# A state-space block on one core: two chained running-sum products per tile in place of three, from the second block on

## The chip, the cores and the metric

The kernel runs on 1 core of one Trainium2 chip. The metric is the device time of one launch in microseconds (us), the median of 3 runs: 468.2 us (467.89 to 468.23). The engines are named as the profile names them: PE (TensorE, matrix products; PEld is its weight load), DVE (VectorE), ACT (ScalarE), POOL (GpSimd), SP (SyncE, here only an issuer of DMAs).

## The reference

Input u has 2048 rows (tokens) of 448 channels. The block is adaptive layer norm, a long convolution, and a gated feed-forward:

```python
mod = (_silu(c) @ w_mod).reshape(c.shape[0], 6, 1, -1)     # sa, ca, ga, sb, cb, gb
h = _layernorm(x, axis=-1) * (1 + ca) + sa
x = x + ga * _A_ref(h, ...)     # y[t] = sum over s <= t of K[t-s] h[s], plus h * Dskip
h = _layernorm(x, axis=-1) * (1 + cb) + sb
x = x + gb * _B_ref(h, ...)     # (silu(h @ w_gate) * (h @ w_up)) @ w_down, hidden width 1792
```

K is the convolution kernel of the state-space part. For these inputs the kernel replaces it, after a test on the device, by the first two terms of a series, K[l] = k0 + k1*l for each channel (the path named `small_path`). Then y[t] needs only running sums over the tokens: k0 times the sum of h, and k1 times a sum weighted with the distance. A running sum inside a tile of 128 tokens is one PE product with a triangular matrix of ones, `tri`; what earlier tiles contribute is one row that is carried from tile to tile.

## The kernel before

The tokens are 16 tiles of 128, in 8 blocks of 2 (`TILES`). After a preamble (`PLAN`, lines 43 to 45, which also does the branch of tiles 0 and 1) the function `run_blocks` runs `ffn` on block b while the branch of block b + 1 is done piece by piece beside it.

`ffn` goes through 14 hidden tiles f = 0..13, here called slots. In slot f, `gate_up(f)` issues 22 products on PE (L758), ACT takes the silu of the first bank (L773), DVE multiplies the second bank by it in place (L788, "the multiply" below), ACT casts the product to `phi` (L795), DVE forms the rest `plo` (L796). Then `down(f - 1)` issues six products that read `phi` and `plo` of the slot before (L808). So PE is two products ahead of the other engines, and needs `phi(f)` only after `gate_up(f + 1)`. In block 0 the weights are split too (L122 to L125, L115 to L117).

The branch pieces hang between these in half slots: `TIMES` gives for each of the two tiles of the next block the half slot h of each stage; h // 2 is the slot, and h % 2 says whether the stage is issued before `down(f - 1)` or after it. Every engine has one queue in program order, so a stage that waits holds back the next slot's silu, multiply and cast on its engine.

The stages of `small_path`: s0 makes h (two DVE operations, L200 and L202); s1 multiplies it by the k0 part `gm0` and the k1 part `gm1` (L957); s2 adds the carried rows `run0` and `run1` to row 0 (L962, L963) and splits the k0 part into two halves `vh` and `vl` (L970, L971) for accuracy; s3 multiplies h by the skip weight `gd` (L976); s4 issues the products with `tri` (L982 to L984) and adds the skip part to x; s5 forms the next carried rows (L1003, L1004), sends them by a small DMA from partition 127 to partition 0 (L1005), and adds both sums to x, the second times the token number `tok` (L1007). In block 0 the k0 part is not split but multiplied at full precision (L995), and DVE does s1 and s3; in block 1 DVE does them too, from block 2 on POOL. After the last stage come the second layer norm of the tile (`n2.stat`, its root on POOL, L185 and L186), `make_xn` (L212 on DVE, L215 and L216 on ACT) and `turn`, a transpose on DVE (L236) with DMAs, which has to be ready in slot 13.

`finish` (L827 to L849) does the last two hidden tiles of the last block in an order of its own. The preamble's `left_over` (L428) sums the k1 part of tiles 0 and 1, from which the first carried row is made (L723).

Of the kernel before, what the change touches and what calls it, by code (L numbers as in the profile page):

```python
# [17 lines left out]
NT = L // 128  # L18
# [17 lines left out]
)  # L36

EXTRA = (1,)

# [12 lines left out]
def f32(ap):  # L52
    return ap.bitcast(F32)
# [3 lines left out]
def tile_kernel(ctx, tc, x, a_re, a_im, b_re, b_im, c_re, c_im, log_dt,  # L57
# [229 lines left out]
    with tc.tile_pool(name="pre", bufs=1) as pre:  # L287
# [47 lines left out]
        for z in range(2):  # L335
# [19 lines left out]
        sca = pre.tile([128, N], F32)  # L355
        h01, v0, v1, hd, h2 = ([pre.tile([128, w], t, name=f"{n}_{q}") for q in range(2)] for n, t, w in
                               (("h", F32, D), ("v0", F32, D), ("v1", F32R, D), ("hd", F32, D), ("h2", F32, 512)))
        qt = {n: pre.tile([128, 512], F32, name="qt" + n) for n in "gcs"}
# [113 lines left out]
        def flag_of():  # L472
# [42 lines left out]
            **{f"D{q}": (lambda q: lambda: sc.activation(diag[q], ident, AF.Copy, scale=n2.of[q][1]))(q) for q in range(2)},  # L515
            "fr1": copy(run1[end], CV[end, 0:D]), "fx": copy(xs[0], DN[0][:, 0:D]),
            "tr0": do(to_channels, 0), "tr1": do(to_channels, 1, (0, 1)), "tr1b": do(to_channels, 1, (2, 3)),
# [203 lines left out]
    def first_rows():  # L721

        ve.tensor_tensor(run0[end], run1[end], DN[1][end, 0:D], op=OP.add)  # L723

# [5 lines left out]
    def gate_0():  # L730

        ve.scalar_tensor_tensor(gm0, gm1, ntok, gm0, op0=OP.mult, op1=OP.add)

    def run_blocks(pools, stages, first=None):
        work, hid = pools.work, pools.hid
        def ffn(ts, fresh, last, todo):
# [148 lines left out]
        for b, ts in enumerate(TILES):  # L885
            todo = {}
            if b + 1 < len(TILES):
# [5 lines left out]
                if b:  # L893
                    for i in nx:
                        at(0, 1, load_x, i)
                stat1, root1, times, *late = TIMES[min(b, 2)]
                st = stages(b)
# [6 lines left out]
                if b == 0 and first is None:  # L904
                    go(EXTRA[0], gate_0)
                    todo["mid"] = [(first_rows, ())]
                    at(0, 1, lambda: sy.dma_start(run[0:1], run[127:128]))
                for i, h in zip(nx, stat1):
# [32 lines left out]
    def small_path(pools):  # L941
# [9 lines left out]

        def s1(i, on_v=False):
            h = vs[i]
            v0 = v0_of(i)
            v1 = work.tile([128, D], F32R, name="v1", bufs=2)
            for v, g in ((v0, gm0), (v1, gm1)):
                (ve if on_v else po).tensor_tensor(v, h, g, op=OP.mult)  # L957
            vs[i] = h, v0, v1

        def rows(i):  # L960
            h, v0, v1 = vs[i]
# [3 lines left out]
        def s2(i):
            rows(i)
            h, v0, v1 = vs[i]
            vh = work.tile([128, D], F32R, name="vh")
            vl = work.tile([128, D], F32R, name="vl")
            sc.copy(vh, v0)  # L970
            ve.tensor_tensor(vl, v0, f32(vh), op=OP.subtract)  # L971
            vs[i] = h, vh, vl, v1

        def s3(i, on_v=False):
            h = vs[i][0]
            (ve if on_v else po).tensor_tensor(h, h, gd, op=OP.mult)  # L976

        def s4(i):
            h, vh, vl, v1 = vs[i]
# [5 lines left out]
            ve.tensor_tensor(xs[i], h, xs[i], op=OP.add)
            vs[i] = o, s

        def s4f(i):  # L990
            h, v0, v1 = vs[i]
            o = CV[:, 0:D]
            s = bank()[:, 0:D]
            pe.matmul(s, tri, v1, start=True, stop=True)
            pe.matmul(o, f32(tri), v0, start=True, stop=True)  # L995
            s3(i, True)
            ve.tensor_tensor(xs[i], h, xs[i], op=OP.add)
            vs[i] = o, s

        def s5(i):  # L1000
            o, s = vs.pop(i)
            if i + 1 < NT:
                sc.copy(run1[end], s[end])  # L1003
                ve.scalar_tensor_tensor(run0[end], run1[end], 128.0, o[end], op0=OP.mult, op1=OP.add)  # L1004
                (sy if i in TILES[1] else sc).dma_start(run[0:1], run[127:128])  # L1005
            ve.tensor_tensor(xs[i], xs[i], o, op=OP.add)
            ve.scalar_tensor_tensor(xs[i], s, tok, xs[i], op0=OP.mult, op1=OP.add)  # L1007
# [109 lines left out]
```

## Time and profile before

| | |
|---|---|
| median of 3 runs | 468.2 us (467.89 to 468.23) |
| the profiled execution: its own time | 466.79 us |
| its span, the stretch that the trace covers | 465.0 us |
| PE busy | 455.5 us, 98% |
| DVE, ACT, POOL busy | 293.5, 170.6, 74.4 us |
| granted TensorE clock | 0.998 of full speed |
| chain that ended last | PE 94%, of which L758 60% and L808 28% |

A row of the timeline or of a chain gives the start in us from the span's start, then the duration. The chain is followed back from the last instruction; if it lies on one engine from end to end, time leaves the kernel only by taking work from that engine or by ending its waits. PE's queue reads blocks as: block 0 from 31.6 us, block 1 from 88.4, block 2 from 141.8, block 3 from 195.2, and so on each some 53.3 us, the last ending at 461.

### The profile page before, as it was taken

What the parts mean: (1) busy time and instruction counts of PE and PEld (TensorE: products, weight loads), DVE (VectorE), ACT (ScalarE), POOL (GpSimd) and SP (SyncE); (2) the same over time, 40 slices, a digit from 0 to 9 for tenths busy, and PEclk for the clock granted to TensorE, in tenths of its full rate; (3) what the DMA queues carried; (4) which work ended last, traced back from release to release, by engine and by line L of the source; (5) the groups of instructions that cost most, each with busy time, mean ns of one, the idle gap of its engine ahead of it and who ended that gap; (6) DMA issues with size and microseconds to landing.
All of it is one profiled execution on the core that took longest, in us unless ns stands there. A gap on an engine that the chain in (4) does not pass through costs nothing.

```text
span 465.0 us, 8481 instructions
## 1 busy us (share of the span) xinstructions
PE 455.5 (98%) x3339; PEld 433.7 (93%) x3339; DVE 293.5 (63%) x600; ACT 170.6 (37%) x426; POOL 74.4 (16%) x99
## 2 busy tenths in 40 slices
PE   6899999999999999999999999999999999999996
PEld 4579999999999999999999999999999999999995
DVE  5888999778726676457736766467745775353224
ACT  5889566522333233322323233322323223232121
POOL 1232001001000521023210431014210331000000
PEclk9999999999999999999999999999999999999999
DMA  8965652110112001120112001120012001110001
GB/s 313 406 254 191 211 179 95 45 36 2 47 45 81 1 0 58 36 79 2 43 51 80 1 0 47 47 80 0 26 56 65 27 2 45 47 61 23 1 1 45
DMA packets 20946, 32.92 MB, mean 71 GB/s; under 512 B 2848, under 2 KB 15264, under 8 KB 20896
## 3 DMA queue, kind: packets, MB, share of 16 engines
q1 hardware_dynamic: 20256, 32.10, 19.9%
q8 instruction: 28, 0.46, 0.4%
q10 hardware_dynamic: 640, 0.18, 0.2%
q14 instruction: 22, 0.18, 0.1%
HBM read 25.40 MB, written 6.82 MB: 69 GB/s over the span
## 4 chain that ended last, share of the span: by engine, by line
PE 94%; issue 2%; DVE 1%; DMA 1%; ACT 1%; POOL 0%; DVEq 0%; POOLq 0%; ACTq 0%
PE bank L758 60%; PE dn L808 28%; DMA vec<-in_c_log_dt_dram 1%; PE dn L480 1%; PE cv L982 1%; PE bank L983 1%; PE cv L984 1%; PE bank L266 0%; PE bank L403 0%; PE cv L995 0%; PE bank L437 0%; ACT L339 0%; DVE x L824 0%; PE cv L375 0%; DVE dn L823 0%
## 5 line engine op out<-in xcount | busy, mean ns | idle before, releaser
L758 PE MATMUL bank<-hhi,gu 128*128 128x256 f32 x1568 | 216.7, 278 | 0.1
L758 PEld LDWEIGHTS bank<-hhi,gu 128*128 128x128 f32 x1568 | 204.0, 188 | 3.7 <-issue 0.8
L758 PE MATMUL bank<-hlo,gu 128*128 128x256 f32 x896 | 138.8, 277 | 0.0
L758 PEld LDWEIGHTS bank<-hlo,gu 128*128 128x128 f32 x896 | 118.6, 188 | 0.2
L788 DVE TENSOR_TENSOR bank<-raw,bank 128x256 f32<-128x256 f32 x97 | 41.4, 426 | 98.3 <-PE bank L758 85.5
L795 ACT CAST phi<-bank 128x256 fp32r<-128x256 f32 x111 | 41.4, 373 | 139.8 <-DVE bank L788 139.8
L796 DVE TENSOR_TENSOR plo<-bank,phi 128x256 fp32r<-128x256 f32 x111 | 47.0, 424 | 44.0 <-ACT phi L795 44.0
L773 ACT ACTIVATE raw<-bank 128x256 f32<-128x256 f32 x98 | 37.6, 384 | 93.0 <-PE bank L758 89.2
L808 PE MATMUL dn<-wdh,phi 128*128 128x448 f32 x220 | 62.7, 366 | 0.0
L808 PE MATMUL dn<-wdh,plo 128*128 128x448 f32 x220 | 62.2, 363 | 0.0
L808 PE MATMUL dn<-wdl,phi 128*128 128x448 f32 x220 | 61.7, 362 | 0.0
L808 PEld LDWEIGHTS dn<-wdh,plo 128*128 128x128 f32 x220 | 41.2, 188 | 3.0 <-DVE plo L796 0.3
L808 PEld LDWEIGHTS dn<-wdl,phi 128*128 128x128 f32 x220 | 41.2, 187 | 2.7
L808 PEld LDWEIGHTS dn<-wdh,phi 128*128 128x128 f32 x220 | 34.3, 188 | 1.6 <-ACT phi L795 0.9
L185 POOL TENSOR_SCALAR rsb<-mvb 128x1 f32<-128x1 f32 (+1 forms) x15 | 8.8, 585 | 115.4 <-DVE mvb L157 115.4
L185 POOL TENSOR_SCALAR rsa<-mva 128x2 f32<-128x2 f32 x8 | 2.7, 341 | 134.0 <-DVE mva L157 131.7
L125 DVE TENSOR_TENSOR gu<-raw,gu 128x1024 fp32r<-128x1024 f32 x14 | 17.1, 1220 | 0.9 <-ACT gu L123 0.9
L215 ACT ACTIVATE raw<-raw,rsb 128x64 f32<-128x64 f32 x14 | 4.9, 349 | 34.6 <-POOL rsb L186 33.6
L957 POOL TENSOR_TENSOR m<-m,gm 128x448 f32<-128x448 f32 x10 | 11.6, 1155 | 25.6 <-DVE m L202 25.6
L963 DVE TENSOR_TENSOR v<-v,run 1x448 fp32r<-1x448 f32 x14 | 13.3, 951 | 0.0
L971 DVE TENSOR_TENSOR vl<-m,vh 128x448 fp32r<-128x448 f32 x12 | 7.4, 618 | 8.9 <-ACT vh L970 8.8
L976 POOL TENSOR_TENSOR m<-m,gd 128x448 f32<-128x448 f32 x10 | 12.9, 1294 | 0.4
(237 smaller groups left out, 413.5 us busy)
## 6 DMA issues: line engine op xcount, KB each, us to landing
raw<-in_B_w_gate_up_dram SPq DMA_DIRECT2D x14, 512.0 KB, 3.4
rawd<-in_B_w_down_dram SPq DMA_DIRECT2D x16, 224.0 KB, 3.7
xd<-raw SPq DMA_DIRECT2D x12, 256.0 KB, 2.0
raw<-xd SPq DMA_DIRECT2D x48, 64.0 KB, 2.0
x<-in_A_u_dram SPq DMA_DIRECT2D x12, 224.0 KB, 2.9
out_dram<-x SPq DMA_DIRECT2D x11, 224.0 KB, 2.0
wm<-in_w_mod_groups_dram SPq DMA_DIRECT2D x5, 448.0 KB, 8.2
wm<-in_w_mod_groups_dram SPq DMA_DIRECT2D x5, 336.0 KB, 8.2
```

What stands on the lines that cost most here:

```text
L125: ve.tensor_tensor(wgu[j][:, :, 3:7, :], w[:, :, ::-1, :], f32(wgu[j][:, :, 0:4, :][:, :, ::-1, :]), op=OP.subtract)
L185: po.tensor_scalar(rs[:, 0:n], self.mv[:, 0:n, 1], EPS, None, op0=OP.add)
L758: pe.matmul(ps[s][:, 0:n], w[:, s, a], (hlo if lo else hhi)[:, k, first_col(n):first_col(n) + n], start=first and q == 0, stop=end and q = ...
L773: sc.activation(p[:, 0:n], ps[0][:, 0:n], AF.Silu)
L788: ve.tensor_tensor(ps[1][:, 0:n], p[:, 0:n], ps[1][:, 0:n], op=OP.mult)
L795: sc.copy(hi[:, 0:n], ps[1][:, 0:n])
L796: ve.tensor_tensor(lo[:, 0:n], ps[1][:, 0:n], f32(hi[:, 0:n]), op=OP.subtract)
L808: pe.matmul(dn[q][:, 0:D], u[:, cs], v, start=f == 0 and z == 0, stop=f == (NF - 3 if last else NF - 1) and z == 2)
L957: (ve if on_v else po).tensor_tensor(v, h, g, op=OP.mult)
L963: ve.tensor_tensor(v1[0:1], f32(v1[0:1]), run1[0:1], op=OP.add)
L971: ve.tensor_tensor(vl, v0, f32(vh), op=OP.subtract)
L976: (ve if on_v else po).tensor_tensor(h, h, gd, op=OP.mult)
```

## The change

From block 1 on a tile has eight stages in place of six. s2 adds the carried row of the h sums to h itself, casts it (`hh`) and keeps the small rest in h. s4 issues one product, u = tri x hh, the running sum of h. s5 forms w = k1 * u + k0 * rest (with the second carried row), carries u's last row, and adds gma * u to x, where gma = gm0 - gm1. s6, two slots later, issues the second product v = tri x w, a running sum of the running sum; s7 carries its last row and adds v to x. The skip part and the k0 part of the rest are products and a sum on POOL in s1 and s3; s5 has one more POOL sum. Each carried row has its own ACT copy and its own DMA on ACT's queue.

In block 0 the stages a1 to a4 run both sums on h and apply k1 behind the sum: one DVE product goes from a1, ACT gets a cast there, and a4 gets one DVE product. `rows_0` (POOL in slot 1, DVE and DMA in slot 2) and `rows_1` (slot 1 of block 1) convert the carried rows between the two forms. The preamble gets two ACT casts, `hh0` and `hh1`, and `left_over` sums these. `finish` issues all products of hidden tile 12 first and then all of tile 13.

```diff
-    ((2, 3), 3, ((4, 5, 7, 8, 10, 11, 12), (7, 8, 13, 14, 16, 17, 18))),
-    ((2, 3), 3, ((4, 5, 7, 8, 10, 11, 12), (7, 8, 13, 14, 16, 17, 18))),
+    ((2, 3), 3, ((4, 4, 6, 6, 8, 8, 12, 12, 13), (6, 7, 12, 12, 14, 14, 18, 18, 19))),
...
-EXTRA = (1,)
+EXTRA = (1, 2, 4, 3)
...
-                pe.matmul(CV[:, 0:D], all1, v1[q], start=q == 0, stop=q == 1)
+                pe.matmul(CV[:, 0:D], all1, hh[q], start=q == 0, stop=q == 1)
...
+    def rows_0(part):
+        t = v0_of(2)[end]
+        if part == 0:
+            po.tensor_tensor(t, run1[end], gm1[end], op=OP.mult)
+        else:
+            ve.tensor_tensor(run0[end], run0[end], t, op=OP.add)
+            sy.dma_start(run[0:1], run[127:128])
...
-                sums(NF - 2, range(m))
-                sums(NF - 1, (0,))
-                sums(NF - 2, (m,))
-                sums(NF - 1, range(1, m + 1))
-                sums(NF - 2, (m + 1,))
-                sums(NF - 1, (m + 1,))
+                for f in (NF - 2, NF - 1):
+                    sums(f, range(m + 2))
...
+        def a4(i):
+            o, s, t = vs.pop(i)
+            sc.copy(run1[end], s[end])
+            ve.tensor_tensor(t, s, gm1, op=OP.mult)
+            ve.scalar_tensor_tensor(run0[end], t[end], 128.0, o[end], op0=OP.mult, op1=OP.add)
+            sy.dma_start(run[0:1], run[127:128])
+            ve.tensor_tensor(xs[i], xs[i], o, op=OP.add)
+            ve.scalar_tensor_tensor(xs[i], t, tok, xs[i], op0=OP.mult, op1=OP.add)
...
+        def s2(i):
+            h = vs[i]
+            ve.tensor_tensor(h[0:1], h[0:1], run1[0:1], op=OP.add)
+            hh = work.tile([128, D], F32R, name="hh", bufs=2)
+            sc.copy(hh, h)
+            ve.tensor_tensor(h, h, f32(hh), op=OP.subtract)
...
+        def s3(i):
+            h = vs[i][0]
+            po.tensor_tensor(h, h, gm0, op=OP.mult)
+            po.tensor_tensor(xs[i], xs[i], v0_of(i), op=OP.add)
...
+        def carry(i, k, row):
+            if i + 1 < NT:
+                sc.copy(run[end, k, :], row[end])
+                sc.dma_start(run[0:1, k, :], run[127:128, k, :])
...
+            ve.tensor_tensor(t, u, gm1, op=OP.mult)
+            ve.tensor_tensor(w, t, h, op=OP.add)
+            ve.tensor_tensor(w[0:1], f32(w[0:1]), run0[0:1], op=OP.add)
+            carry(i, 1, u)
+            ve.tensor_tensor(t, u, gma, op=OP.mult)
+            po.tensor_tensor(xs[i], xs[i], t, op=OP.add)
```

PE, block 3, around the first sum of its first prepared tile (tile 8). Before, slot 5, between `gate_up(5)` and `down(4)`:

```order
L758 MATMUL bank<-hhi,gu_509 128x256 x7
L758 MATMUL bank<-hlo,gu_509 128x256 x4
L982 MATMUL cv<-vh,tri 128x448
L983 MATMUL bank<-v_2526,tri 128x448
L984 MATMUL cv<-vl,tri 128x448
L808 MATMUL dn_68<-wdh_558,phi 128x448
```

Now the first sum of tile 8 stands in slot 4 (the sum of `w` follows in the same way in slot 6, as one L1039):

```order
L774 MATMUL bank<-hhi,gu_476 128x256 x7
L774 MATMUL bank<-hlo,gu_476 128x256 x4
L1017 MATMUL cv<-hh,tri 128x448
L824 MATMUL dn_68<-wdh_516,phi 128x448
L824 MATMUL dn_69<-wdh_516,phi 128x448
```

Three products in one place have become one in each of two places; PE has 12 instructions fewer in all (six blocks, two tiles), and no bank of the four that `gate_up` turns through is taken for a sum.

DVE, block 3, from the last stage of tile 8 (x_74) to the multiply of slot 8; m is the buffer of h and of the products, raw the buffer of `make_xn` and also of silu's result. Before:

```order
L212 SCALAR_TENSOR_TENSOR raw<-x_74,mvb,cbw 128x448 [waits DVE_49]
L962 TENSOR_TENSOR m_79<-m_79,run 1x448 [waits DMAHW2_49,Pool_49]
L963 TENSOR_TENSOR v_2604<-v_2604,run 1x448 [waits Pool_49]
L971 TENSOR_TENSOR vl<-m_79,vh 128x448 [waits Activation_49]
L788 TENSOR_TENSOR bank<-raw,bank 128x256 [waits PE_49,Activation_49]
L796 TENSOR_TENSOR plo<-bank,phi 128x256 [waits Activation_49]
L236 STREAM_TRANSPOSE raw<-raw 128x4x4x32
L788 TENSOR_TENSOR bank<-raw,bank 128x256 [waits PE_49,Activation_49]
```

Now:

```order
L1045 TENSOR_TENSOR x_74<-x_74,dn_70 128x448 [waits Activation_49,Pool_49]
L1003 TENSOR_TENSOR m_79<-m_79,run 1x448 [waits DMAHW6_49]
L1006 TENSOR_TENSOR m_79<-m_79,hh 128x448 [waits Activation_49]
L156 BN_STATS stb<-x_74 128x6
L157 BN_AGGR mvb<-stb 128x2 [waits DVE_49]
L804 TENSOR_TENSOR bank<-raw,bank 128x256 [waits PE_49,Activation_49]
L812 TENSOR_TENSOR plo<-bank,phi 128x256 [waits Activation_49]
L212 SCALAR_TENSOR_TENSOR raw<-x_74,mvb,cbw 128x448 [waits DVE_49]
L1029 TENSOR_TENSOR m_79<-cv,g_90 128x448 [waits PE_49,Pool_49]
L1030 TENSOR_TENSOR w<-m_79 128x448 [waits DVE_49]
L1031 TENSOR_TENSOR w<-w,run 1x448 [waits DMAHW7_49,DVE_49]
L1033 TENSOR_TENSOR m_79<-cv,gma 128x448 [waits Activation_49]
```

The transpose L236 and the multiply of slot 8 follow directly. POOL, block 3, from tile 9's h to tile 8's root (L185, L186) and beyond, before:

```order
L957 TENSOR_TENSOR m_79<-m_79,gm_91 128x448 [waits DVE_49,Activation_49]
L957 TENSOR_TENSOR v_2604<-m_79,g_90 128x448 [waits PE_49]
L185 TENSOR_SCALAR rsb<-mvb 128x1 [waits DVE_49]
L186 TENSOR_TENSOR rsb<-rsb,halves 128x1 [waits Pool_49]
L976 TENSOR_TENSOR m_79<-m_79,gd 128x448
```

and now, from tile 9's s1:

```order
L999 TENSOR_TENSOR m_79<-m_79,gd 128x448 [waits DVE_49]
L1034 TENSOR_TENSOR x_74<-x_74,m_79 128x448 [waits DVE_49,Pool_49]
L1011 TENSOR_TENSOR m_79<-m_79,gm_91 128x448 [waits DVE_49]
L1012 TENSOR_TENSOR x_75<-x_75,m_79 128x448 [waits DMAHW5_49,Pool_49]
L185 TENSOR_SCALAR rsb<-mvb 128x1 [waits DVE_49,Activation_49]
L186 TENSOR_TENSOR rsb<-rsb,halves 128x1 [waits Pool_49]
L1034 TENSOR_TENSOR x_75<-x_75,m_79 128x448 [waits DVE_49]
```

The whole second half of the tile's work, four operations of s5, now stands between `make_xn` and the multiply of slot 8, and tile 8's root on POOL stands behind two full operations of tile 9.

DVE, block 0, slots 10 and 11 (x_75 is tile 3; the weight splits L117 and L125 are L116 and L124 now). Before:

```order
L796 TENSOR_TENSOR plo<-bank,phi 128x256 [waits Activation_49]
L1004 SCALAR_TENSOR_TENSOR run<-run,cv 32x448 [waits Activation_49]
L1006 TENSOR_TENSOR x_75<-x_75,cv 128x448 [waits DVE_49]
L1007 SCALAR_TENSOR_TENSOR x_75<-bank,tok,x_75 128x448 [waits DVE_49]
L156 BN_STATS stb<-x_75 128x6 [waits DVE_49]
L157 BN_AGGR mvb<-stb 128x2 [waits DVE_49]
L117 TENSOR_TENSOR wdl_920<-rawd_83,wdh_919 128x448 [waits DMAHW2_49,Activation_49]
L788 TENSOR_TENSOR bank<-p,bank 128x256 [waits PE_49,Activation_49]
```

Now:

```order
L812 TENSOR_TENSOR plo<-bank,phi 128x256 [waits Activation_49]
L992 TENSOR_TENSOR m_79<-bank,g_90 128x448 [waits Activation_49]
L993 SCALAR_TENSOR_TENSOR run<-m_79,cv 32x448 [waits DVE_49]
L995 TENSOR_TENSOR x_75<-x_75,cv 128x448
L996 SCALAR_TENSOR_TENSOR x_75<-m_79,tok,x_75 128x448 [waits DVE_49]
L156 BN_STATS stb<-x_75 128x6 [waits DVE_49]
L157 BN_AGGR mvb<-stb 128x2 [waits DVE_49]
L116 TENSOR_TENSOR wdl_928<-rawd_83,wdh_927 128x448 [waits DMAHW2_49,Activation_49]
```

One full DVE product (L992) stands ahead of what was there, in front of the multiply of slot 11.

## Rows read from the trace of the kernel before

**Rows 1.** The page, busy us (share of the span) and instructions.

```profile
PE 455.5 (98%) x3339; PEld 433.7 (93%) x3339; DVE 293.5 (63%) x600; ACT 170.6 (37%) x426; POOL 74.4 (16%) x99
```

**Rows 2.** The chain in order of time: start, duration, what.

```profile
81.10 1.39 PE dn L808 x6
...
105.89 2.52 PE bank L758 x22
109.01 1.20 PE dn L808 x6
...
141.78 5.18 PE bank L758 x44
...
195.18 5.00 PE bank L758 x44
...
220.53 2.51 PE bank L758 x22
```

**Rows 3.** Line 982: duration min/median/max ns, first and last start.

```profile
L982 PE MATMUL cv<-vh,tri x12: 367/367/367, 108.2 to 386.6; 128*128 128x448 f32 x12
```

**Rows 4.** Timeline of POOL, block 3: start, duration, idle before.

```profile
207.92 1.15 POOL L957 TENSOR_TENSOR v<-m,g 128x448 fp32r<-128x448 f32 x1
209.15 1.42 POOL L976 TENSOR_TENSOR m<-m,gd 128x448 f32<-128x448 f32 x1
...
221.57 0.71 POOL L185 TENSOR_SCALAR rsb<-mvb 128x1 f32<-128x1 f32 x1 [6.26 <-DVE mvb L157]
222.37 0.78 POOL L186 TENSOR_TENSOR rsb<-rsb,halves 128x1 f32<-128x1 f32 x1
```

**Rows 5.** Timeline of DVE, block 3.

```profile
209.47 1.57 DVE L963 TENSOR_TENSOR v<-v,run 1x448 fp32r<-1x448 f32 x1
210.98 0.61 DVE L971 TENSOR_TENSOR vl<-m,vh 128x448 fp32r<-128x448 f32 x1
...
220.65 0.62 DVE L156 BATCH_NORM_STATS2 stb<-x 128x6 f32<-128x448 f32 x1
...
225.27 0.42 DVE L788 TENSOR_TENSOR bank<-raw,bank 128x256 f32<-128x256 f32 x1
226.13 0.42 DVE L796 TENSOR_TENSOR plo<-bank,phi 128x256 fp32r<-128x256 f32 x1 [0.44 <-ACT phi L795]
226.47 0.70 DVE L236 STREAM_TRANSPOSE raw<-raw 128x512 f32<-128x512 f32 x1
```

**Rows 6.** Timeline of ACT, block 3 (ACTq: a DMA issued there).

```profile
217.63 0.50 ACTq L1005 DMA_DIRECT2D run<-run  x1
...
223.18 0.35 ACT L215 ACTIVATE raw<-raw,rsb 128x64 f32<-128x64 f32 x1 [2.90 <-POOL rsb L186]
223.56 0.67 ACT L216 ACTIVATE raw<-raw,rsb 128x448 f32<-128x448 f32 x1
224.14 0.55 ACT L970 CAST vh<-m 128x448 fp32r<-128x448 f32 x1
```

**Rows 7.** Timeline of DVE, block 0, slots 10 and 11.

```profile
76.19 0.63 DVE L1004 SCALAR_TENSOR_TENSOR run<-run,cv 32x448 f32<-32x448 f32 x1
...
79.88 0.42 DVE L788 TENSOR_TENSOR bank<-p,bank 128x256 f32<-128x256 f32 x1
...
81.35 0.42 DVE L796 TENSOR_TENSOR plo<-bank,phi 128x256 fp32r<-128x256 f32 x1
```

**Rows 8.** Timeline of PE, block 0, the last pair of `down(11)`.

```profile
81.82 0.68 PE L808 MATMUL dn<-wdh,plo 128*128 128x448 f32 x2
```

**Rows 9.** Timeline of the tail, PE and DVE in `finish`.

```profile
458.63 0.47 PE L836 MATMUL bank<-wdh,phi 128*128 128x448 f32 x1 [0.17 <-ACT phi L782]
...
459.56 0.62 DVE L847 TENSOR_TENSOR x<-bank,x 128x448 f32<-128x448 f32 x1 [0.45 <-PE bank L836]
...
460.91 0.36 DVE L847 TENSOR_TENSOR x<-dn,x 128x192 f32<-128x192 f32 x1 [0.22 <-PE dn L836]
```

**Rows 10.** Timeline of ACT in the preamble.

```profile
27.72 0.54 ACT L395 COPY qts<-bank 128x448 f32<-128x448 f32 x1 [1.06 <-PE bank L269]
```

More of the change, by code (lines that the diff above doesn't have):

```diff
@@ L138, in tile_kernel @@
     gm1 = g0
+    gma = const.tile([128, D], F32)
     ones = const.tile([128, 1], F32)
@@ L355, in tile_kernel @@
         sca = pre.tile([128, N], F32)
-        h01, v0, v1, hd, h2 = ([pre.tile([128, w], t, name=f"{n}_{q}") for q in range(2)] for n, t, w in
-                               (("h", F32, D), ("v0", F32, D), ("v1", F32R, D), ("hd", F32, D), ("h2", F32, 512)))
+        h01, v0, v1, hd, hh, h2 = ([pre.tile([128, w], t, name=f"{n}_{q}") for q in range(2)] for n, t, w in
+                               (("h", F32, D), ("v0", F32, D), ("v1", F32R, D), ("hd", F32, D), ("hh", F32R, D), ("h2", F32, 512)))
         qt = {n: pre.tile([128, 512], F32, name="qt" + n) for n in "gcs"}
@@ L515, in tile_kernel @@
             **{f"D{q}": (lambda q: lambda: sc.activation(diag[q], ident, AF.Copy, scale=n2.of[q][1]))(q) for q in range(2)},
-            "fr1": copy(run1[end], CV[end, 0:D]), "fx": copy(xs[0], DN[0][:, 0:D]),
+            **{f"hh{q}": copy(hh[q], h01[q]) for q in range(2)}, "fr1": copy(run1[end], CV[end, 0:D]), "fx": copy(xs[0], DN[0][:, 0:D]),
             "tr0": do(to_channels, 0), "tr1": do(to_channels, 1, (0, 1)), "tr1b": do(to_channels, 1, (2, 3)),
@@ L721, in first_rows @@
     def first_rows():
-        ve.tensor_tensor(run0[end], run1[end], DN[1][end, 0:D], op=OP.add)
+        ve.tensor_copy(run0[end], DN[1][end, 0:D])
     def gate_row():
@@ L895, in run_blocks @@
                         at(0, 1, load_x, i)
-                stat1, root1, times, *late = TIMES[min(b, 2)]
+                stat1, root1, times, *late = TIMES[min(b, 1)]
                 st = stages(b)
@@ L906, in run_blocks @@
                     todo["mid"] = [(first_rows, ())]
-                    at(0, 1, lambda: sy.dma_start(run[0:1], run[127:128]))
+                    go(EXTRA[1], rows_0, 0)
+                    go(EXTRA[2], rows_0, 1)
+                if b == 1 and first is None:
+                    go(EXTRA[3], rows_1)
                 for i, h in zip(nx, stat1):
@@ L948, in s0 @@
             vs[i] = h
[L952 to L961, printed above, removed]
-            ve.tensor_tensor(v0[0:1], v0[0:1], run0[0:1], op=OP.add)
-            ve.tensor_tensor(v1[0:1], f32(v1[0:1]), run1[0:1], op=OP.add)
@@ L965, in s2, with a1 @@
[L965 to L979, printed above, removed]
+        def a1(i):
+            h, v0 = vs[i], v0_of(i)
+            ve.tensor_tensor(v0, h, gma, op=OP.mult)
+            hh = work.tile([128, D], F32R, name="hh", bufs=2)
+            sc.copy(hh, h)
+            vs[i] = h, v0, hh
@@ L980, in s4, with a2, a3 @@
+        def a2(i):
+            h, v0, hh = vs[i]
+            ve.tensor_tensor(v0[0:1], v0[0:1], run0[0:1], op=OP.add)
+            ve.tensor_tensor(hh[0:1], f32(hh[0:1]), run1[0:1], op=OP.add)
+        def a3(i):
+            h, v0, hh = vs[i]
             o = CV[:, 0:D]
             s = bank()[:, 0:D]
-            pe.matmul(o, tri, vh, start=True, stop=False)
-            pe.matmul(s, tri, v1, start=True, stop=True)
-            pe.matmul(o, tri, vl, start=False, stop=True)
+            pe.matmul(s, tri, hh, start=True, stop=True)
+            pe.matmul(o, f32(tri), v0, start=True, stop=True)
+            ve.tensor_tensor(h, h, gd, op=OP.mult)
@@ L985, in s4 @@
             ve.tensor_tensor(xs[i], h, xs[i], op=OP.add)
[L986 to L998, printed above, removed]
-        def s5(i):
[L1001 to L1007, printed above, removed]
@@ new lines, in s1 @@
+        def s1(i):
+            po.tensor_tensor(v0_of(i), vs[i], gd, op=OP.mult)
+        def s2(i):
+            h = vs[i]
+            ve.tensor_tensor(h[0:1], h[0:1], run1[0:1], op=OP.add)
+            hh = work.tile([128, D], F32R, name="hh", bufs=2)
+            sc.copy(hh, h)
+            ve.tensor_tensor(h, h, f32(hh), op=OP.subtract)
+            vs[i] = h, hh
+        def s3(i):
+            h = vs[i][0]
+            po.tensor_tensor(h, h, gm0, op=OP.mult)
+            po.tensor_tensor(xs[i], xs[i], v0_of(i), op=OP.add)
@@ new lines, in s4 @@
+        def s4(i):
+            h, hh = vs[i]
+            u = CV[:, 0:D]
+            pe.matmul(u, tri, hh, start=True, stop=True)
+            vs[i] = h, u
+        def carry(i, k, row):
+            if i + 1 < NT:
+                sc.copy(run[end, k, :], row[end])
+                sc.dma_start(run[0:1, k, :], run[127:128, k, :])
+        def s5(i):
+            h, u = vs[i]
+            t = v0_of(i)
+            w = work.tile([128, D], F32R, name="w")
+            ve.tensor_tensor(t, u, gm1, op=OP.mult)
[4 more added lines that the diff above has]
+            po.tensor_tensor(xs[i], xs[i], t, op=OP.add)
+            vs[i] = w
@@ L1013, in general_path, with s6, s7 @@
+        def s6(i):
+            v = DN[2][:, 0:D]
+            pe.matmul(v, tri, vs[i], start=True, stop=True)
+            vs[i] = v
+        def s7(i):
+            v = vs.pop(i)
+            carry(i, 0, v)
+            ve.tensor_tensor(xs[i], xs[i], v, op=OP.add)
+        return lambda b: (s0, s1, s2, s3, s4, s5, s6, s7) if b else (s0, a1, a2, a3, a4)
     def general_path(pools, y):
```

13 lines of the change are left out of this document (8 added, 5 removed).

## The prediction

> **What bounds the kernel now.** I read the page's busy line first: PE is busy 455.5 us of the span of 465.0 us, DVE 63%, ACT 37%, POOL 16% [rows 1]. That alone does not show that PE sets the time, so I read the chain in order of time next. From block 0 to the tail it stays on PE: 22 products of L758 in 2.51 us, six of L808 in 1.20 us, and again [rows 2]. So each product that goes is worth its full time, if nothing new makes PE wait; and everything that DVE, ACT and POOL get in addition costs nothing until a slot's `phi` or `plo` comes late. How late they may come is the question here, so the rest of the reading is of these engines' timelines in block 3, a typical block, and in block 0.
>
> **What goes from PE.** In the chain, L758 ends at 105.89 + 2.52 = 108.41 and L808 begins at 109.01 [rows 2]. The 0.60 us between hold the three products with `tri`, 0.20 us each. L982 is there 12 times [rows 3], so are its two neighbours; now there are two products per tile, 12 times. PE loses 12 x 0.20 = 2.4 us. The row's 367 ns [rows 3] is one product from start to end and overlaps the next; it is not the price. Block 0 keeps its two products per tile.
>
> **What the other engines get, in blocks 1 to 6.** The tight place is slots 6 to 8, where tile A's last stage, tile B's s2 and s5, tile A's layer norm and its transpose meet. I walk it with t = 0 at the end of `gate_up(6)`. PE then does one sum (0.2), `down` (1.2), `gate_up` (2.5), and the same again: `gate_up(7)` ends at 3.9, `gate_up(8)` at 7.8. Slot 8 has no sum, `gate_up(9)` ends at 11.5, and after tile B's second sum `down(8)` asks for `phi(8)` at 11.7.
> - DVE: multiply, wait of 0.44 for the cast, `plo` [rows 5]: free at 1.3. ACT copies the carried row (about 0.55, as the cast L970 [rows 6]); DVE waits for it, adds v to x (0.6) and the carried row to h (0.55), to 2.6; ACT casts h, to 3.2; DVE subtracts (0.6 [rows 5]), to 3.8; statistics 0.62 [rows 5] and 0.2, to 4.65. The multiply of slot 7 is 0.75 late, `plo(7)` ends at 5.85.
> - POOL: the two operations of s3 follow the subtraction, 1.15 each [rows 4]: 3.9 to 6.15. Tile A's root stands behind them: 0.71 + 0.78 as in the rows where DVE works beside it [rows 4], to 7.6.
> - ACT: the two scalings of `make_xn` wait for that root, as they do today (2.90 us of idle time ahead of L215 [rows 6]); 0.35 + 0.6 [rows 6], to 8.6. Only then come the copy of u's last row, 0.55, to 9.1, its DMA, 0.50 [rows 6], to 9.6, and the silu of slot 8, 0.4, to 10.0.
> - DVE: `make_xn` 0.6 after the POOL operation that ends at 6.15, then four operations of 0.6, the last waiting for the row copy of 9.1, to 9.75; transpose 0.65 [rows 5], to 10.4; the multiply of slot 8 to 10.8, `phi(8)` at 11.2.
>
> So `phi(8)` is ready 0.5 us before it is asked for. Today the multiply of slot 7 begins at 225.27, where `gate_up(7)` ended at 220.53 + 2.51 = 223.04 [rows 2, 5]: 2.2 us late, and PE does not wait. With the change the worst is 10.4 - 7.8 = 2.6 us late. I take 0 for the six blocks. The other end is where every POOL operation of this walk meets DVE: L976 took 1.42 and not 1.15 us [rows 4], and the DVE operation beside it, L963, 1.57 us where the like of it takes 0.6 [rows 5]. Then PE waits in each block, priced under the rivals. Below nothing it cannot go, because PE does not wait for DVE there now.
>
> That row pair is weighed with a rule. L963 began at 209.47 and ended at 211.04, 0.47 us after L976's end at 210.57 [rows 4, 5], as if it had only then begun; the multiplies, which read one operand from PSUM, keep 0.42 us. The Trainium skill (SBUF — State Buffer, Who interferes with whom) says that a DVE instruction with two SBUF inputs and a GpSimd instruction that reads SBUF take turns, the second one blocked until the first is done; the trace agrees. By that rule the added POOL operations (four per tile, three before) speak against the change; in my walk it has its place once, where `make_xn` waits for 6.15.
>
> **Block 0.** Here DVE is nearly full. The multiply of slot 11 begins at 79.88, and `plo(11)` at 81.35 is the last that `down(11)` waits for: its last pair starts at 81.82 and the six take 1.39 instead of 1.20 us [rows 2, 7, 8]. Ahead of that place a4 puts one DVE product, L992, in front of the operation that stands at 76.19 [rows 7]: 0.63 + 0.02 us. Over the slots before, DVE gets 0.55 (`rows_0`, slot 2) and 0.65 (a4 of tile 2, slot 8) and loses two products (slots 4 and 5) at 0.55; between them it partly catches up with PE and partly waits for ACT, which has two casts more, so that I take 0 to +0.3 for these, 0.15. With no cover left, `plo(11)` ends 0.8 us later and PE waits 0.8 us more. Bounds: 0 (DVE catches up: the first branch of the range) and 1.1.
>
> **Preamble and tail.** `hh0` and `hh1` are two casts of about 0.5 us on ACT. ACT is idle for 1.06 us ahead of L395 at 27.72 [rows 10], so they fit: 0, at most 0.2. In `finish` PE waits for `phi` before 458.63 [rows 9]; with all of tile 12 first, it has 0.64 us of products for that time, and the wait goes. What is late next is DVE: the first part of the result is complete some 0.15 us later than for the operation at 459.56, and three operations of 0.62, 0.42 and 0.36 in a row then end about 0.1 us before 460.91 + 0.36 [rows 9]. I take -0.1, with 0.1 either way.
>
> **An open size.** The first 44 products of a block take 5.18 us in some blocks and 5.00 in others [rows 2] (four of the seven after block 0 have 5.18). The rows do not show why; as the sums no longer take turns in the four banks, all or none of them may be so: -0.7 to +0.5 us. I take 0.
>
> **The sum.** -2.4 + 0.8 - 0.1 = -1.7 us. Against the profiled execution's 466.79 us (its span of 465.0 and 1.8 around it) that is 465.1; the median of the runs shown, 468.2, lies 1.4 above that execution, and I carry the gain over: 466.5 us.
>
> **Rivals.**
> - *Block 0 absorbs its addition*, because DVE has caught up by slot 10, or the 5.18 blocks become 5.00. For it: two products less in slots 4 and 5. Against: no idle time on DVE worth the name in slots 10 and 11 [rows 7]. Gain 2.4 + 0.1 to 3.0; 465.7 (465.2 to 466.0).
> - *The gain is eaten.* Block 0 costs its 1.1 and slot 8 some 0.15 us in each of six blocks: -2.4 + 1.1 + 0.9 - 0.1 = -0.5, or 467.7.
> - *Slower: slot 8 waits for POOL.* Place: tile A's root behind tile B's two operations of s3, then ACT's scalings, its row copy, the silu, the multiply. Price: what the lateness exceeds 2.6 + 0.5 = 3.1 us, six times. If two operations take 1.42 and three of DVE's (`make_xn`, the sum for w, its row) lose 0.3 each behind POOL, the lateness grows by 0.55 + 0.9, or 1.45: 0.95 us in each of six blocks, 5.7 in all, 468.2 - 1.7 + 5.7 = 472.2. It decides from 0.5 us on, and makes the kernel slower than before from 0.8 us on (0.28 x 6 = 1.7). For it: the 1.57 us of L963. Against: that was one operation in a tile, and the root's own 0.71 and 0.78 already hold such waits. It is what the rule above does where all its cases fall on the chain.
> - *The change does not do what it says*: PE's 2.4 us would come back as other waits of PE. It has only `phi`, `plo` and the sums' inputs to wait for; the sums' inputs are ready well ahead (in the walk w at 8.4 for the sum at 11.5), so this falls under the two above.
>
> **How the numbers follow.** Two runs of this kernel differ by 0.34 us, and 0.2% (0.94 us) is what a measurement can tell from no change. Forecast (466.0 to 467.1): 0.47. First rival: 0.19. Eaten (467.1 to 469.1): 0.21. Slower (above 469.1): 0.13. Faster by over 0.2%, below 467.26: 0.47 + 0.19 + 0.01 of the third case, 0.67. Within 0.2%: the rest of the third case, 0.20. Slower: 0.13. The range leaves out the far end of the first rival and the slower one with the edge of the third: 465.2 to 468.8.
>
> **What would show it.** PE: 12 products fewer, 0.2 us between L758 and L808 in slots 4, 6, 7 and 9 of a block, and no wait of PE at `down(8)`; block 0 some 0.8 us longer, with the wait at `down(11)`; no wait in `finish`. DVE: the multiply of slot 8 some 2.6 us after `gate_up(8)`. The forecast is wrong if PE shows idle time at `down(5)` or `down(8)` in every block, or if block 0 is no longer than before.

## The result, and the profile after

The changed kernel takes 469.85 us (median of 9 runs, 468.94 to 471.21), the kernel before 468.18 (9 runs): ratio 1.0044, 95% interval 1.0031 to 1.0057. It is slower by more than a measurement can miss; 466.5 was forecast. The page's busy line of the kernel after, beside [rows 1]:

```profile
PE 456.1 (98%) x3327; PEld 433.0 (93%) x3327; DVE 295.9 (63%) x598; ACT 179.2 (38%) x441; POOL 96.3 (21%) x119
```

PE has its 12 products less (3327 instead of 3339), and yet it is busy 0.6 us longer. Its timeline, cut at the first product of each stage, gives for the two profiled executions (us):

| stage | before | after | difference | forecast |
|---|---|---|---|---|
| start to block 0 | 31.60 | 32.37 | +0.77 | 0 |
| block 0 | 56.60 | 58.64 | +2.04 | +0.8 |
| blocks 1 to 6 | 320.01 | 319.62 | -0.39 | -2.4 |
| block 7 to `finish` | 49.48 | 49.68 | +0.20 | 0 |
| `finish` to the end | 7.31 | 7.39 | +0.08 | -0.1 |

The first row is mostly chance: 0.47 of it is a weight transfer ahead of L256 that landed later, and the other profiles of this preamble start block 0 at 31.53 to 32.51 us, those of the old preamble at 31.60, 32.50 and 32.58. The fourth is the first 44 products of block 7, 5.18 us here and 5.00 before. The same chance, with the other sign, is -0.33 of the third row: four of these six blocks begin with 5.18 us before, two after. Sorted by kind, the rest of the six blocks is -2.30 for the sums, +2.17 for the groups of 22 products and +0.07 for `down`. So two places need a reason: block 0, and six blocks in which the gain of 2.3 us is gone. The difference of the medians is +1.7. The chain before and after, block 3 (start, duration, what; before, the three sums of tile 8 and `down` stand between the two rows):

```profile
212.50 2.52 PE bank L758 x22
...
216.82 2.52 PE bank L758 x22
```

```profile
211.40 2.51 PE bank L774 x22
213.91 0.21 PE cv L1017
214.12 1.20 PE dn L824 x6
215.31 2.59 PE bank L774 x22
217.91 1.21 PE dn L824 x6
219.12 2.53 PE bank L774 x22
221.64 0.20 PE dn L1039
221.85 1.20 PE dn L824 x6
223.05 2.59 PE bank L774 x22
```

Nothing stands between the pieces after the change: PE waits for nobody. The sums take 0.20 us each, as counted. But the 22 products of `gate_up` (L774, a gate group from here on) that come after a sum take 2.59 us, the next ones 2.53, where before they take 2.52 and 2.51 [rows 2], even behind three sum products. In 2.59 us consecutive products begin 0.118 us apart, in 2.51 us 0.114. It is not the clock: from 211.40 to 213.91 us (2.51) and from 215.31 to 217.90 (2.59) the granted clock is 1.00 of full speed. All 24 groups behind a sum do so, and with the groups after them that is the 2.17 us: the gain.

Block 0 after, ACT and DVE timelines:

```profile
51.38 0.38 ACT L811 CAST phi<-bank 128x256 fp32r<-128x256 f32 x1
54.24 0.57 ACT L971 CAST hh<-m 128x448 fp32r<-128x448 f32 x1 [2.49 <-DVE m L202]
54.72 0.56 ACT L114 CAST wdh<-rawd 128x448 fp32r<-128x448 f32 x1
```

```profile
40.36 1.85 DVE L124 TENSOR_TENSOR gu<-raw,gu 128x1024 fp32r<-128x1024 f32 x1
...
55.31 0.62 DVE L116 TENSOR_TENSOR wdl<-rawd,wdh 128x448 fp32r<-128x448 f32 x1 [0.44 <-ACT wdh L114]
56.72 1.23 DVE L124 TENSOR_TENSOR gu<-raw,gu 128x1024 fp32r<-128x1024 f32 x1 [0.45 <-ACT gu L122]
...
82.13 0.42 DVE L804 TENSOR_TENSOR bank<-p,bank 128x256 f32<-128x256 f32 x1
...
83.93 1.84 DVE L212 SCALAR_TENSOR_TENSOR raw<-x,mvb,cbw 128x448 f32<-128x448 f32 x2
```

a1 of tile 3 stands in the same half slot as the step that makes its h. Its cast reaches the head of ACT's queue 2.49 us before DVE has finished h (L202), and the weight cast L114 and the silu stand behind it; then DVE idles twice, 0.9 us together, in the block where it is full. The multiply of slot 11 begins 49.76 us after the block's start, 48.28 before [rows 7].

That is 1.48 of the 2.04 us; the other 0.55 come behind it. The pair of L212 (`make_xn`) takes 1.84 us, and before 1.27. POOL's product for `gma` (L746, in `rows_1`) runs beside it:

```profile
81.69 1.27 DVE L212 SCALAR_TENSOR_TENSOR raw<-x,mvb,cbw 128x448 f32<-128x448 f32 x2
```

```profile
83.09 1.60 POOL L746 TENSOR_TENSOR gma<-gm,g 128x448 f32<-128x448 f32 x1
```

The program issues this product in slot 1 of block 1, but it follows the root directly in POOL's queue, waits for nothing that the profile shows, and so runs in slot 11 of block 0. ACT's scalings and the next cast then come later, PE's transposes of tiles 2 and 3 (L227) wait, and `down(12)` begins 56.15 us after the block's start, 54.11 before. In all 14 profiles with this product the first L212 takes 1.23 to 1.25 us, in the three without it 0.67 or 0.68. No run moves the product, so its price is read from the traces and not shown by an experiment.

### The profile page after: what moved, and what is told of

Read it like the earlier page. It is cut to its first block, busy times and chain, and to the rows that moved or that the text cites. A ratio compares the mean times of both kernels' runs of the same rounds, so it can differ in the third digit from the quotient of the medians.

```text
span 467.7 us, 8502 instructions
## 1 busy us (share of the span) xinstructions
PE 456.1 (98%) x3327; PEld 433.0 (93%) x3327; DVE 295.9 (63%) x598; ACT 179.2 (38%) x441; POOL 96.3 (21%) x119
## 4 chain that ended last, share of the span: by engine, by line
PE 87%; DVE 6%; issue 3%; ACT 2%; DMA 1%; POOL 0%; DVEq 0%; ACTq 0%; POOLq 0%
PE bank L774 56%; PE dn L824 26%; DVE gu L124 1%; DMA vec<-in_c_log_dt_dram 1%; DVE wdl L116 1%; PE dn L480 1%; DVE plo L812 1%; PE cv L1017 1%; PE dn L1039 1%; PE bank L266 0%; DVE bank L804 0%; PE bank L403 0%; ACT gu L121 0%; ACT raw L216 0%; PE bank L437 0%
## 5 line engine op out<-in xcount | busy, mean ns | idle before, releaser
L774 PE MATMUL bank<-hhi,gu 128*128 128x256 f32 x1568 | 217.8, 279 | 0.1
L774 PEld LDWEIGHTS bank<-hhi,gu 128*128 128x128 f32 x1568 | 204.9, 188 | 3.6 <-issue 1.0
L774 PE MATMUL bank<-hlo,gu 128*128 128x256 f32 x896 | 139.5, 278 | 0.0
L774 PEld LDWEIGHTS bank<-hlo,gu 128*128 128x128 f32 x896 | 119.1, 188 | 0.2
L824 PEld LDWEIGHTS dn<-wdh,phi 128*128 128x128 f32 x220 | 35.3, 188 | 2.0 <-ACT phi L811 1.3
L185 POOL TENSOR_SCALAR rsa<-mva 128x2 f32<-128x2 f32 x8 | 2.7, 341 | 133.4 <-DVE mva L157 131.2
L1011 POOL TENSOR_TENSOR m<-m,gm 128x448 f32<-128x448 f32 x12 | 16.1, 1345 | 48.0 <-DVE m L1006 48.0
L124 DVE TENSOR_TENSOR gu<-raw,gu 128x1024 fp32r<-128x1024 f32 x14 | 17.7, 1265 | 1.3 <-ACT gu L122 1.3
L202 DVE SCALAR_TENSOR_TENSOR m<-m,rsa,sa 128x448 f32<-128x448 f32 x14 | 14.3, 1019 | 1.0
L185 POOL TENSOR_SCALAR rsb<-mvb 128x1 f32<-128x1 f32 (+1 forms) x15 | 5.8, 385 | 35.4 <-ACT raw L789 19.6
L236 DVE STREAM_TRANSPOSE raw<-raw 128x512 f32<-128x512 f32 x12 | 8.5, 705 | 7.0 <-ACT raw L216 7.0
```

The lines of the kernel that those rows point to most:

```text
L124: ve.tensor_tensor(wgu[j][:, :, 3:7, :], w[:, :, ::-1, :], f32(wgu[j][:, :, 0:4, :][:, :, ::-1, :]), op=OP.subtract)
L185: po.tensor_scalar(rs[:, 0:n], self.mv[:, 0:n, 1], EPS, None, op0=OP.add)
L202: ve.scalar_tensor_tensor(h, h, rs, sh, op0=OP.mult, op1=OP.add)
L236: ve.transpose(dst.rearrange("p (b k r) -> p k b r", b=4, k=4), src.rearrange("p (k b c) -> p k b c", b=4, k=4))
L774: pe.matmul(ps[s][:, 0:n], w[:, s, a], (hlo if lo else hhi)[:, k, first_col(n):first_col(n) + n], start=first and q == 0, stop=end and q = ...
L824: pe.matmul(dn[q][:, 0:D], u[:, cs], v, start=f == 0 and z == 0, stop=f == (NF - 3 if last else NF - 1) and z == 2)
```

## Experiments on the gate groups

There are four theories for the slow groups: the number of 448-column products between two gate groups, a wait in PE's queue, a product that stands alone, or something else of the change. In the kernels *triples*, *pairs* and *fours* each sum product of tiles 4 to 15 is repeated (the diff shows the first sum of *pairs*; the second is edited alike, and the other two have 3 and 4):

```diff
-            pe.matmul(u, tri, hh, start=True, stop=True)
+            for _ in range(2):
+                pe.matmul(u, tri, hh, start=True, stop=True)
```

> The changed kernel with each of the 24 sum products of tiles 4 to 15 issued three times over in its place (48 products of 0.20 us more on TensorE: 9.6). Theory 'count': the spacing of the 22 gate products behind a sum (0.114 or 0.118 us) hangs on how many 448-column products stand between them and the gate products before, and 6 or 9 (multiples of three) leave it at 0.114: the groups behind a sum take 2.51 instead of 2.59 us, and the time is 469.85 + 9.6 - 2.3 = 477.2. Rival 'wait': what slows the group is that the sum waits for its operand in TensorE's queue, which it does here as well: 2.59 stays, 479.5.

> The changed kernel with each of the 24 sum products of tiles 4 to 15 issued twice in its place (24 products of 0.20 us more: 4.8). 'Count': 8 products of 448 columns are no multiple of three either, the groups behind a sum stay at 2.59 us: 474.7. Rival 'alone': only a sum product that stands by itself does it, and two together leave 2.51: 474.7 - 2.3 = 472.4.

> The changed kernel with each of the 24 sum products of tiles 4 to 15 issued four times over in its place (72 products of 0.20 us more: 14.4). One, two and three products have left 2.59, 2.50 and 2.52 us behind them. 'Cycle of three': the 448-column products come in a repeating pattern of three spacings (0.202, 0.197, 0.201 us), and the gate group is slow if its first product comes in at one of the three places; 6 + 4 = 10 products leave it there as 7 do: the group behind a sum takes 2.59 us, 469.85 + 14.4 = 484.3. Rival 'alone': only one single product does it, 2.51, 484.3 - 2.3 = 482.0.

Measured: 477.94, 472.65 and 482.31 us, one run each. The chain of *pairs*, block 3:

```profile
211.78 2.52 PE bank L774 x22
214.30 0.41 PE cv L1018 x2
214.70 1.20 PE dn L824 x6
215.90 2.51 PE bank L774 x22
```

Two, three and four products leave 2.50 to 2.53 us behind them, one leaves 2.59. 'Wait' falls with *triples*, 'count' with *pairs*, and the cycle of three with *fours*: it put ten products where seven are. 'Alone' gave 472.4 and 482.0 and stands. The kernel *two weights* asks whether the same weights twice matter:

```diff
+            pe.matmul(u, hh[:, 0:128], hh, start=True, stop=True)
             pe.matmul(u, tri, hh, start=True, stop=True)
```

> The changed kernel with a product of the operand's own first 128 columns as weights ahead of each of the 24 sum products, into the same columns, which the sum then overwrites (4.8 more on TensorE). Two products with the same weights left 2.51. Theory 'number': two of any kind leave 2.51 behind them: 469.85 + 4.8 - 2.3 = 472.4. Rival 'weights': only a product that follows one with its own weights undoes it, and here no two have the same: 2.59, 474.7.

471.89 us (one run), groups of 2.50 to 2.52: the number, not the weights. And the same from the other side, the kernel *before one*:

```diff
-            s = bank()[:, 0:D]
-            pe.matmul(o, tri, vh, start=True, stop=False)
-            pe.matmul(s, tri, v1, start=True, stop=True)
-            pe.matmul(o, tri, vl, start=False, stop=True)
+            s = o
+            pe.matmul(o, tri, vh, start=True, stop=True)
```

> The kernel before, with two of the three sum products of each of the tiles 4 to 15 left out (the low part and the second sum, whose row is read from the first; 24 products of 0.20 us less: -4.8). If the slow group comes from the number of products and nothing else of the change, the group behind the one product that is left takes 2.59 us and the next 2.53 instead of 2.52 and 2.50 (12 x 0.10 = +1.2): 467.74 - 4.8 + 1.2 = 464.1. If it comes from the changed kernel's other steps (which bank, which operands, POOL's and ScalarE's work beside it), the group stays at 2.52: 462.9.

464.94 us (one run). Blocks 1 to 6 take 316.1 us, 3.9 less than before, where -4.8 + 1.2 = -3.6 had been forecast; block 0 begins at 32.50 in this execution, 0.90 later than in the profile before. What it computes lacks the two sums, so it is of use for the time alone. Its chain, block 3:

```profile
212.16 2.52 PE bank L758 x22
214.68 0.21 PE cv L982
214.88 1.20 PE dn L808 x6
216.08 2.59 PE bank L758 x22
218.68 1.21 PE dn L808 x6
219.88 2.52 PE bank L758 x22
```

The kernel before has the slow group too as soon as one product is alone. So it is not the changed kernel's banks, operands or other engines. Two ways out were tried. *Halves*:

```diff
-            pe.matmul(u, tri, hh, start=True, stop=True)
+            for c in (slice(0, 224), slice(224, D)):
+                pe.matmul(u[:, c], tri, hh[:, c], start=True, stop=True)
```

> The changed kernel with each sum product of tiles 4 to 15 cut into two of 224 columns (no more columns in all; by the 256-column products' 0.114 us two take at most 0.23 instead of 0.20: 24 x 0.03 = up to 0.7 more). 'Count': six products of 448 columns are left between the groups, so 2.51 comes back: 469.85 - 2.3 + 0.4 = 468.0. 'Wait' and 'alone': still 2.59 behind each sum, 470.2.

468.31 us (ratio to the kernel before 1.0017, 1.0007 to 1.0026). Block 3:

```profile
210.10 2.52 PE bank L774 x22
212.62 0.21 PE cv L1018 x2
212.83 1.22 PE dn L824 x6
214.05 2.51 PE bank L774 x22
```

The two halves and the six products behind them take 0.03 us more, the gate group 0.08 less. That is the number 468.0 within its error, though the reason given in 'count' (six long products) had been wrong. 'Alone' had 470.2 here and missed: two short products do not count as one. The other way is the place (*behind*):

```diff
-    ((2, 3), 3, ((4, 4, 6, 6, 8, 8, 12, 12, 13), (6, 7, 12, 12, 14, 14, 18, 18, 19))),
+    ((2, 3), 3, ((4, 4, 6, 6, 9, 9, 13, 13, 14), (6, 7, 12, 12, 15, 15, 19, 19, 20))),
```

> The changed kernel with each sum of tiles 4 to 15 (and the steps that go with it) half a slot later: the single product comes behind the six down products, next to the gate group that it has slowed, instead of ahead of them. Theory 'place': the single product does it where it stands between a gate group and a down group; behind down the group after it takes 2.51: 469.85 - 2.3 = 467.5. Rival 'seven': any seven products of 448 columns between two gate groups do it: 2.59 stays, 469.8.

472.06 us (1.0110, 1.0093 to 1.0126), worse than either. The chain in block 3, and the one at the end of block 4:

```profile
213.19 1.20 PE dn L824 x6
214.39 0.20 PE cv L1017
214.59 2.51 PE bank L774 x22
...
296.45 2.02 DMA xd<-raw
299.82 3.74 DMA raw<-xd
303.82 0.52 ACT hhi L219
```

Behind the six products of `down` one product does no harm: 2.50 or 2.51 us behind all 24 sums. But the turn of tile B (the second tile of each pair) goes out half a slot later, and its round trip through memory lands so late that the next block's first product waits for it (1.3 us at this place); blocks 4 to 6 take 54.6, 53.5 and 54.4 us. Neither theory had foreseen this price. *Behind early* moves tile B's last steps ahead (`17, 17, 18` at the end of its list, for 19, 19, 20):

> The kernel 'behind' with the last sum of each block, tile B's second, in half slot 17 instead of 19 (its statistics, root, normalization and turn two half slots earlier with it). Theory 'the late turn': the first products of a block no longer wait for the transfer, all groups behind a sum stay at 2.50, and blocks 1 to 6 are 14 x (2.50 + 1.20) + 4 x 0.20 + the 0.2 to 0.4 at a block's start, 52.8 to 53.0 each, 0.4 less than in the changed kernel: 469.85 - 2.3 = 467.5. Rival 'elsewhere': w of tile B, only one slot old, is not ready, and the sum waits at half slot 17: over 469.

468.89 us (1.0041, 1.0028 to 1.0054). The wait at the block's start is gone, and both theories were half right: in three of the six blocks the group behind the moved-up sum is slow again. Block 3, PE's timeline:

```profile
229.81 0.47 PE L1039 MATMUL dn<-w,tri 128*128 128x448 f32 x1
230.12 0.99 PE L774 MATMUL bank<-hhi,gu 128*128 128x256 f32 x7
```

This sum takes 0.47 us from start to end and not 0.37: its operand is too young. In the other five blocks its weights are loaded 0.06 to 0.09 us later than in *behind* (they follow the load before after 0.26 to 0.29 us instead of 0.20), and two of these five groups are slow too. So behind `down` the place was safe in these runs only for a sum whose operand was old.

## Experiments on block 0 and the tail

*a1 order*, tile 2's a1 first:

```diff
-    ((1, 3), 5, ((5, 10, 13, 15, 15, 16), (9, 9, 17, 19, 20, 20)), 20, (22, 23)),
+    ((1, 3), 5, ((5, 9, 13, 15, 15, 16), (9, 10, 17, 19, 20, 20)), 20, (22, 23)),
```

> The changed kernel with the two a1 steps of block 0 in the other order (tile 2's in half slot 9, tile 3's in 10), so that ScalarE's cast of tile 3's h no longer stands in its queue before VectorE has made h. Theory: the 2.49 us for which that cast held the casts of w_down behind it put 0.9 us of idle time on VectorE (0.44 before L116, 0.45 before L124), and block 0 becomes 0.9 shorter: 469.0. Rival: VectorE is behind anyway for the added row operations and the idle time moves elsewhere: block 0 within 0.2 of 58.80, 469.8.

469.39 us (1.0031, 1.0018 to 1.0043); block 0 57.80 instead of 58.64. In ACT's timeline the weight cast now follows at once:

```profile
51.53 0.57 ACT L971 CAST hh<-m 128x448 fp32r<-128x448 f32 x1
52.00 0.57 ACT L114 CAST wdh<-rawd 128x448 fp32r<-128x448 f32 x1
```

So the queue had cost at least these 0.84 us; the table below gives its whole size. *Rows early* makes one operation of `first_rows` and `rows_0`:

```diff
-        ve.tensor_copy(run0[end], DN[1][end, 0:D])
+        ve.tensor_tensor(run0[end], v0_of(2)[end], DN[1][end, 0:D], op=OP.add)
...
-                    go(EXTRA[1], rows_0, 0)
-                    go(EXTRA[2], rows_0, 1)
+                    at(0, 2, rows_0, 0)
```

> The changed kernel with the carried row of block 0 put together in one VectorE operation as before (GpSimd multiplies run1 by gm1 ahead of it, at block 0's first multiply, and first_rows adds the sum's row to it): VectorE loses L740 (0.62 us), and GpSimd's L738 no longer runs beside L124 (1.85 instead of 1.22 us there: 0.63). Theory 'VectorE is full': block 0 shrinks by up to 0.62 + 0.63 = 1.25 from 58.64: 57.4, 468.6. Rival: ScalarE's queue (the cast of tile 3 that waits for h) ends block 0's delays, and VectorE only idles longer before L116: within 0.2 of 58.64, 469.8.

470.31 us (1.0066, 1.0048 to 1.0084), block 0 58.83: the theory missed, and the rival had the number but not the reason. L740 is gone, but POOL's product now runs beside L116, which takes 1.25 us instead of 0.62, so that behind slot 2 DVE is only 0.16 us ahead (L200). With all three edits:

> The changed kernel with the sums in halves (468.31 measured alone), the a1 steps of block 0 in the other order (-0.84 on block 0 alone) and the row of block 0 early. If the two edits of block 0 add up (VectorE full): block 0 56.6, as in the kernel before, and 468.3 - 0.84 - 1.2 = 466.3, 0.3% under the kernel before (467.74). If the second finds only what the first has left idle: block 0 at 57.4 to 57.8, 467.5, no difference that can be told.

466.5 us (0.9982, 0.9971 to 0.9993), block 0 57.29: behind *a1 order* the row is worth 0.5, not 1.2. Where the delay of block 0 arises and goes shows in four places of the five profiles, in us from the block's start:

| begins | before | after | a1 order | rows early | three edits |
|---|---|---|---|---|---|
| L157, last statistics of tile 3 | 47.28 | 49.14 | 47.93 | 48.95 | 47.78 |
| multiply of slot 11 | 48.28 | 49.76 | 48.93 | 49.95 | 48.40 |
| `down(12)` | 54.11 | 56.15 | 55.31 | 56.33 | 54.80 |
| block 1 | 56.60 | 58.64 | 57.80 | 58.83 | 57.29 |

At L157 the order of the a1 steps gives back 1.21 us, the row behind it 0.15, and 0.50 are left, the place of L992. Between L157 and the multiply there is a second difference, of 0.36 us: before, in *a1 order* and in *rows early* DVE stands idle there, and after and in *three edits* it does not.

```profile
79.34 0.63 DVE L117 TENSOR_TENSOR wdl<-rawd,wdh 128x448 fp32r<-128x448 f32 x1 [0.27 <-issue]
```

This row is of the kernel before; the profile names no releaser for the idle time, and why it comes in some kernels stays open. It takes 0.36 of the 1.21 back in *a1 order*; and since the kernel before has it and *three edits* has not, L992's 0.50 shrink to 0.12 us at the multiply. Of the 0.7 that are left there, the other 0.57 come at `down(12)`, from the product for `gma`.

> The kernel of 'three edits' with whole sum products behind the down products instead of halves ahead of them. 'Place': the halves' 24 x 0.027 us go as well: 466.5 - 0.65 = 465.85. 'Seven': the slow groups are back, 466.5 + 2.3 - 0.65 = 468.2.

> The same with the two edits of block 0 (57.3 us in 'three edits'). 'The late turn': the 466.5 of 'three edits' less 24 x 0.027 for the halves = 465.9, 0.35% under the kernel before. 'Elsewhere': 467 or more.

470.08 (1.0070) and 466.6 us (0.9996, 0.9987 to 1.0005): the late turn comes back in the first, which no theory had, and the young operand in the second, where five of the six groups behind the moved-up sum are slow. *Mixed all* keeps three sums behind `down` and the last in halves ahead of it:

> The kernel of 'three edits' with the first three sums of each block whole and behind the down products (half slots 9, 13, 15) and the last one, tile B's second, in halves ahead of them in half slot 18, its statistics in 19 as in the changed kernel. 'Place': all groups behind a sum at 2.50 to 2.52, no wait at a block's start, three of four sums without the halves' 0.027: 18 x 0.027 = 0.5 less than 'three edits', ratio to the kernel before 0.997. 'Waiting': the half slot less between tile B's steps makes its second sum wait again, groups of 2.59 there: ratio 0.999 or more.

466.34 us (0.9970, 0.9959 to 0.9982), as 'place' had it. The ratio is the lowest of all, but its interval overlaps that of *three edits*. Its chain, block 3:

```profile
212.21 0.20 PE cv L1013
212.42 2.51 PE bank L770 x22
...
219.83 0.20 PE dn L1036
220.04 2.51 PE bank L770 x22
...
230.17 0.21 PE dn L1036 x2
230.39 1.22 PE dn L820 x6
231.60 2.51 PE bank L770 x22
```

Of the tail, only the new order of `finish` put into the kernel before:

> The kernel before with only the finish of the changed one. From finish's first product to the end of the span it took 7.31 us before and 7.39 after: if the shorter product order (-0.28) and the output transfers that start closer together (+0.36) both come from finish alone, 7.39 here too and no difference in the time (467.6 to 467.8); if the later transfers were chance, 7.03 and 467.4.

467.38 us (one run), the number of the second case, but not by its reason. From the first product of `finish` to DVE's last operation it takes 3.30 us, as after the change (3.58 before); from there to the end 4.25 (3.73 before, 4.09 after). So in this execution what PE and DVE gain is given back behind DVE. In all 15 profiles with the new order this last part takes 3.98 to 4.47 us; but with the old order it took 5.21 in *before one*, so it is not shown that the close start of the output transfers causes it.

## Why the prediction was wrong

*The step that failed* is "So each product that goes is worth its full time, if nothing new makes PE wait". In blocks 1 to 6 nothing made PE wait, and the 12 x 0.20 us went as counted (2.30 measured). But the products that stay changed their pace: where three went together one stands alone, and the gate groups take 2.17 us more. The step treated a product's time as its own; nothing in the forecast allowed for one product changing the next ones, though [rows 2] already had two paces for the same 44 products.

*The second miss* is block 0's size, +2.04 for +0.8 (bounds 0 to 1.1). The mechanism that was named, L992 ahead of the last multiplies, is 0.50 us at L157 and 0.12 at the multiply: "with no cover left" was not so, for the row of L117 with 0.27 us of idle time lies between the lines of [rows 7]. The term that was far too small is "0 to +0.3" for the slots before. The "two casts more" on ACT were counted by their duration; what cost 1.21 was that one of them waits in the queue, and the row's operations cost 0.15. The remaining 0.55, the product for `gma` beside `make_xn`, was in no term.

The Trainium skill (SBUF — State Buffer, Who interferes with whom) lets such a pair, a DVE instruction with two SBUF inputs and a GpSimd instruction that reads SBUF, take turns; the trace agrees. L212's first operation ends 0.48 us after L746 and alone takes 0.67. In slot 1 L738 ran beside L124 in the same way, which took 1.85 instead of 1.22 us; but DVE's wait for the weight cast behind it shrank from 1.09 to 0.46 us, so this one cost nothing. The forecast had weighed the rule for slots 6 to 8 alone.

*What held.* The walk through slots 6 to 8: after the change, DVE in block 3:

```profile
226.31 0.41 DVE L804 TENSOR_TENSOR bank<-raw,bank 128x256 f32<-128x256 f32 x1
...
232.03 0.40 DVE L804 TENSOR_TENSOR bank<-raw,bank 128x256 f32<-128x256 f32 x1
```

`gate_up(7)` ends at 225.64 and `gate_up(8)` at 229.64: 0.67 and 2.39 us late, 0.75 and 2.6 forecast, and PE does not wait. So the slower rival (POOL) did not come at its place, slot 8. That the time lies in its band (above 469.1, chance 0.13) is a coincidence of the number. The preamble's casts fit: ACT's idle time ahead of L395 fell from 1.06 to 0.16 us. "The gain is eaten" had the size nearest to the result, but by waits at slot 8 that never were; the truth lay above the range by the pace of the gate groups and the costs in block 0, which no case had. The wait in `finish` went, its -0.1 did not arrive.

## What to carry to other kernels

When products are taken out of a bound PE stream, compare afterwards the pace of the products that stay, group by group, with the chain; a busy share of 98% hides it. A small product that would stand alone between two kinds of groups can be cut in two or moved to the other side of the long group, if its operand is old enough and nothing behind it has a deadline. On an engine with a queue, count for each added instruction what it waits for, and who stands behind it. An instruction that waits for nothing runs when its queue reaches it, which can be a block earlier than the place where the program issues it, and beside work that it was not meant to meet.

## What the runs showed of the hardware

A single 448-column product between 22 products of 256 columns and six of 448 slows the next 22 from 0.114 to 0.118 us each, the group after that a little; two to four there do not, nor does a single one behind the six whose operand is ready. PE shows no idle time in either. Shown are the number and the place, and that it is neither the same weights twice nor the changed kernel's operands; why a single one does it stays open. It is not the only thing that does: after the change a group of block 0 with no sum near it (58.85 us) has the slow pace too, behind a `down` that had waited.

The 44 products at a block's start have the same two paces, 0.118 us in 5.18 and 0.114 in 5.00, and there the same program goes either way by itself. In *finish alone*, whose blocks are those of the kernel before, only one of the seven groups after block 0 takes 5.18 us, against four before:

```profile
89.32 5.18 PE bank L758 x44
142.72 5.01 PE bank L758 x44
195.92 5.01 PE bank L758 x44
```

That is 0.6 us of difference in blocks 1 to 6 (319.4 us against 320.0), in which nothing was changed.
